# A two-layer GQA decode block: a reordered end, wider value steps and a table gelu

## The chip, the cores and the metric

The kernel runs on one NeuronCore of a Trainium2 chip. The metric is the device time of one execution in microseconds. Of the kernel before there are five runs: 306.32, 307.86, 307.25, 308.18 and 310.83 us, median 307.86. The profiled execution is the one of 306.32 us.

## The reference

Two layers of attention and of a gated FFN, with the same weights and the same caches in both layers, for one new token in each of four batch elements. x is 4 x 512, there are 32 query heads and 8 key/value heads of 128, and each cache holds 4096 positions per head; all in bfloat16.

```python
def _A_ref(x, k_cache, v_cache, wq, wo):
    q = (x @ wq) as heads
    k, v = caches, each head repeated 4 times
    scores = einsum("bhqd,bhkd->bhqk", q, k) * (Dh ** -0.5)
    o = einsum("bhqk,bhkd->bhqd", softmax(scores), v)
    return o @ wo
def _B_ref(x, w_gate, w_up, w_down):
    return (gelu(x @ w_gate) * (x @ w_up)) @ w_down    # tanh form, F = 1792

x = x + _A_ref(_layernorm(x), ...)      # twice over:
x = x + _B_ref(_layernorm(x), ...)      # attention, FFN, attention, FFN
```

## The kernel before, in words

**What moves.** K and V of one batch element are 8 MB each. The K tiles of an element stay in SBUF for both layers, so K is read once; V passes through seven buffers of 512 KB (`KV_BUFS`) and is read in both layers, but for two tiles of element 0 (`keep`). Weights are read once. All transfers are issued from SP, in the order in which the code calls `dma_start`; a V load waits until the matmuls that read its buffer's last tile are done, a K load until the scores that read the old tile are done.

**The pipeline over elements.** `attend(b2, b1)` runs the second layer's attention of element b2 = b beside the first layer's of element b1 = b + 1. Between two calls lies `dense(b, ...)`, the FFN of the first layer for one element: the second layer of an element needs its result. So the order for each element is: V steps of the first layer, out projection, `dense`, layer norm, q projection, K scores of the second layer; those scores free the K tiles for the next element's K loads. `attend_last` does the second layer of element 3, and the code behind it runs the second layer's FFN for all four elements at once and writes the output.

**V steps.** `Values.step` (L486) takes one V tile: 16 matmuls (L501), each with a 128 x 128 block of V as weights and four probability columns repeated `WIDE` = 8 times, 32 columns. A pass has 16 steps. The result's first copy is scaled into `OT_bf` on DVE (L509). `fill` in `dense` puts V steps of an earlier element between the FFN's stages, so that PE has work and V buffers come free. For element 0 there are no such steps, and `fill` calls `keep_clock(n)` (L342): n matmuls of 512 columns whose result nobody reads; `waits` gives the numbers. `down` (L349) repeats H's columns in the same manner, up to 32.

**The FFN and the norms.** `add_y` (L301) adds a result to x and accumulates its sum, `ln_square` (L165) the sum of squares; `ln_center` multiplies both with a constant matrix on PE to get mean and mean square in all partitions (L177) and subtracts the mean; `ln_rstd` (L193 to L208) finds 1/sqrt with integer arithmetic and two Newton steps on DVE. The gate and up projections (L314) leave rows that DVE turns into columns (L223). `gelu` is the tanh form: DVE operations around one ACT tanh (L328); `gate_up` multiplies with (tanh + 1) and with the up projection into `H_bf` (L340).

**The out projection.** Most heads go through `out_proj` into rows, which DVE turns and copies to `yc` (L269); `y_select` (L276) adds the rows up on PE (the row sums); the last heads are added directly by `out_proj_end` (L294).

**Softmax.** `soft` is a maximum on DVE and an exp on ACT (L418), `soft_turn` a turn on DVE (L426), `soft_swap` 16 matmuls and an ACT copy to `pe` (L445, L448), `soft_den` and `soft_recip` the denominators.

The schedule is written by hand: each engine runs its instructions in the order of the code. The functions that the change touches, with the profile's line numbers:

Of the kernel before, what the change touches and what calls it, by code (L numbers as in the profile page):

```python
# [15 lines left out]
P = 128  # L16
# [14 lines left out]
def kernel(  # L31
# [29 lines left out]
    WIDE = 8  # L61
# [40 lines left out]
    xo = state.tile([P, QS], BF16, name="xo")  # L102
    xr = state.tile([QS, P], BF16, name="xr")
# [6 lines left out]
    magic = const.tile([P, B], I32, name="magic")  # L110
    s32_f = const.tile([P, QS], FP32, name="s32_f")
# [30 lines left out]
    def build_consts():  # L142
        nc.vector.memset(mean_f[:], 1.0 / D)
        nc.vector.memset(magic[:], 0x5F3759DF)
        for r in ROWS:
            nc.vector.memset(r[:], 0.0)
        nc.vector.memset(qb[:], 0.0)
        nc.vector.memset(xo[:], 0.0)
        nc.vector.tensor_reduce(out=amask[:], in_=ident_bf[:].rearrange("p (a i) -> p a i", a=QD),
                                axis=AX.X, op=ALU.max)  # L150
        nc.vector.tensor_reduce(out=s32_f[:], in_=ident_bf[:].rearrange("p (a i) -> p i a", a=QD),
                                axis=AX.X, op=ALU.max)
        nc.vector.tensor_copy(out=t32_bf[:],
                              in_=s32_f[:].unsqueeze(1).broadcast_to([P, QD, QS]))
        nc.vector.tensor_reduce(out=hmask[:], in_=s32_f[:].rearrange("p (y h) -> p h y", h=rep),
                                axis=AX.X, op=ALU.max)
        nc.vector.scalar_tensor_tensor(
            out=dmask[:], in0=amask[:].unsqueeze(2).broadcast_to([P, GH, rep]), scalar=float(D),
            in1=hmask[:].unsqueeze(1).broadcast_to([P, GH, rep]), op0=ALU.mult, op1=ALU.mult)
# [12 lines left out]
    def ln_center(b0, nb):  # L172
        bs = slice(b0, b0 + nb)
        mv = small.tile([P, 2, nb], FP32, name="mv", tag="mv")
        if nb == 1:
            st = ps_sm.tile([P, 2, 1], FP32, name="st", tag="sm")
            nc.tensor.matmul(st.rearrange("p s o -> p (s o)"), lhsT=mean_f[:, :], rhs=sums[:],  # L177
                             start=True, stop=True)
            nc.vector.tensor_scalar(out=xn_bf[:, :, b0], in0=XX[:, 0, b0], scalar1=st[:, 0],
                                    scalar2=None, op0=ALU.subtract)  # L180
            nc.vector.tensor_copy(out=mv[:], in_=st[:])
            return mv
# [7 lines left out]

    def ln_rstd(nb, mv):
        msq = small.tile([P, nb], FP32, name="msq", tag="msq")
# [125 lines left out]
    def ffn_cols(rows, nb):  # L318
        return turn_rows(rows, KF * QS)[:, :, :nb]

    def gelu(nb, hg, rstd, sq, h):
# [8 lines left out]
                                       in1=spread_rstd(rstd, n, nb), op0=ALU.mult, op1=ALU.mult)  # L330

    def ffn_tiles(nb):
        sq = small.tile([P, KF, nb], FP32, name="sq", tag="sq")
        h = small.tile([P, KF, nb], FP32, name="h", tag="h")
        return sq, h, small.tile([P, KF, nb], BF16, name="H_bf", tag="H_bf")

    def gate_up(hu, sq, h, H_bf):
        nc.vector.scalar_tensor_tensor(out=sq[:], in0=sq[:], scalar=1.0, in1=h[:],
                                       op0=ALU.add, op1=ALU.mult)
        nc.vector.tensor_tensor(out=H_bf[:], in0=hu, in1=sq[:], op=ALU.mult)  # L340
# [8 lines left out]
    def down(nb, H_bf, between=()):  # L349
        n = WIDE * rep // nb  # L350
        y = ps_sm.tile([P, KD, n, nb], FP32, name="y", tag="sm")
        for c in range(KF):
            if c in between:
                keep_clock(between[c])
            for k in range(KD):
                nc.tensor.matmul(y[:, k], lhsT=wd_sb[:, c, k * P:(k + 1) * P],  # L356
                                 rhs=H_bf[:, c, :].unsqueeze(1).broadcast_to([P, n, nb]),
                                 start=(c == 0 and k == 0), stop=(c == KF - 1), skip_group_check=True)
        return y[:, :, 0]
# [103 lines left out]
    keep = {(0,) + u[2:] for u in value_order(0, 1)[:KEEP]}  # L463
# [18 lines left out]
    class Values:  # L482
# [3 lines left out]
        def step(self, count=1):  # L486
            for _ in range(min(count, VB - self.n)):
# [4 lines left out]
                pe, rden = self.prob[g]  # L492
                if self.n % (2 * NT) == 0:
                    self.ot = ps_ot.tile([P, 2, WIDE, rep], FP32, name="ot", tag="ot")
# [3 lines left out]
                for i in range(CH):  # L498
                    c = t * CH + i
                    rhs = pe[:, s, c, :].unsqueeze(1).broadcast_to([P, WIDE, rep])  # L500
                    nc.tensor.matmul(self.ot[:, s % 2], lhsT=v[:, i, :], rhs=rhs,  # L501
# [16 lines left out]
    def attend(b2, b1, next_q=None, rest=None):  # L518
# [78 lines left out]
        vals.step(2)  # L597
# [10 lines left out]
        vals.step(3)  # L608
        soft_turn(p0)
        if not first:  # L610
            for i in range(2):
                out_proj(rows, OT_bf, heads[i], hp, i == 0)
        pe, den = soft_swap(p0, p1p), soft_den(p0)
        if two:
            p1 = soft(sc2[1])
        prob1[gb] = (pe, soft_recip(den))
        vals.step(3)
        if two:
            soft_turn(p1)
            pe1, den1 = soft_swap(p1, p2p), soft_den(p1)  # L620
            prob2[gb] = (pe1, soft_recip(den1))
        if first:
# [7 lines left out]
            return (y, OT_bf, heads[3], hp), vals2  # L630
        vals.step()
        keep_clock(1)
        vals.step()
        out_proj(rows, OT_bf, heads[2], hp)
        vals.step()
# [9 lines left out]
    def attend_last(b2, next_q, rest):  # L645
# [27 lines left out]
        prob2[gb] = (soft_swap(p0, p2p), soft_recip(soft_den(p0)))  # L673
        out_proj(rows, OT2_bf, heads[0], hp, True)
# [7 lines left out]
        vals.step()  # L682
        y = y_select(yc, B)
        vals.step()
        return y, OT2_bf, heads[5], rep

    def dense(b0, nb, proj, fill, between=()):
# [4 lines left out]
        ln_square(b0, nb)  # L692
        mv = ln_center(b0, nb)
# [7 lines left out]
        gate_up(ffn_cols(ru, nb), sq, h, H_bf)  # L701
        fill(2)
        add_y(b0, nb, down(nb, H_bf, between))
# [4 lines left out]
    for b in range(B):  # L708
        if prev is None:
            waits = iter((1, 5, 6, 2, 1, 0, 3, 1))  # L710
# [3 lines left out]
        dense(b, 1, proj, fill, {KF // 2: 1, KF - 4: 1} if prev is None else ())  # L714
        ln_square(b, 1)
        fill(1)
        mv = ln_center(b, 1)
# [20 lines left out]
    def ffn_part(w_sb, h, c0, c1):  # L738
        for c in range(c0, c1):
            for k in range(KD):  # L740
# [6 lines left out]
    ln_square(0, B)  # L747
    mv = ln_center(0, B)
    banks = [new_rows(), new_rows()] + [new_scores(i).rearrange("p c j -> p (c j)")
                                        for i in range(NG)]  # L750
    hg, hu = [[t[:, :KF * B].rearrange("p (c j) -> p c j", j=B) for t in banks[i::2]]
              for i in range(2)]
    parts = [(0, KF // 2), (KF // 2, KF)]
    rstd = ln_rstd(B, mv)
    for i, (c0, c1) in enumerate(parts):
        ffn_part(wg_sb, hg[i], c0, c1)
    sq, h, H_bf = ffn_tiles(B)
    for i, (c0, c1) in enumerate(parts):
        gelu(B, hg[i][:, c0:c1], rstd, sq[:, c0:c1], h[:, c0:c1])
    for i, (c0, c1) in enumerate(parts):  # L760
        ffn_part(wu_sb, hu[i], c0, c1)
        gate_up(hu[i][:, c0:c1], sq[:, c0:c1], h[:, c0:c1], H_bf[:, c0:c1])
    y = down(B, H_bf)
    nc.vector.tensor_tensor(out=xo[:, :B * KD].rearrange("p (b k) -> p b k", k=KD),
                            in0=XX[:, 0], in1=y.rearrange("p k b -> p b k"), op=ALU.add)
    for a in range(QD):
        nc.vector.transpose(out=xr[:, a * QS:(a + 1) * QS], in_=xo[a * QS:(a + 1) * QS, :])
    nc.sync.dma_start(out=out.flatten_outer_dims().rearrange("b (k c) -> (b k) c", k=KD),
                      in_=xr[:B * KD, :])
# [30 lines left out]
```

## Time and profile before

| | |
|---|---|
| median of five runs | 307.86 us |
| profiled execution | 306.32 us |
| its span (first to last instruction) | 304.5 us |
| PE busy | 199.1 us, 65% |
| DVE busy | 172.3 us, 57% |
| ACT busy | 29.3 us, 10% |
| HBM read | 113.51 MB, 373 GB/s over the span |
| mean granted TensorE clock | 0.748 |

The page cuts the span into 40 slices of 7.6 us, each digit the busy share in tenths. PEclk is the granted clock of TensorE in tenths of full speed. The chain follows the work that ended last backwards, at each step to what released it; `SPq` is time in SP's queue, "issue" time in which an engine waited for nothing that the profile shows. PEld are the weight loads, which overlap the matmuls. In a timeline or group, `64x` or `x64` stands for so many instructions that are shown together, the time being that of the whole stretch.

### The profile page before, as it was taken

How to read it: one execution, taken by the hardware profiler on the slowest of the kernel's cores; microseconds unless marked ns; L12 is line 12 of the kernel's file. 1: busy time of each engine (PE TensorE's matmuls, PEld its weight loads, DVE VectorE, ACT ScalarE, POOL GpSimd, SP SyncE). 2: the span in 40 equal slices, each digit the busy share in tenths (PEclk: the TensorE clock that was granted, in tenths of full speed). 3: DMA queues.
4: the chain of work that ended last, by engine and by line, in shares of the span. 5: the costliest groups of instructions: out<-in, count | busy, mean ns of one | idle time of the engine just before them, and what ended most of it. 6: DMA issues, size and time to landing. Idle time of an engine off the chain costs nothing.

```text
span 304.5 us, 8771 instructions
## 1 busy us (share of the span) xinstructions
PE 199.1 (65%) x3865; PEld 118.1 (39%) x3873; DVE 172.3 (57%) x490; ACT 29.3 (10%) x71; POOL 0.7 (0%) x6
## 2 busy tenths in 40 slices
PE   1334385346767548788855387998562878988874
PEld 1011144112424125556431245564311555635654
DVE  6496841014258987465478953555799543545144
ACT  0003010000002021300100212001002130003100
POOL 0000000000000000000000000000000000000000
PEclk9998576557798558997965578799655795679685
DMA  7999999999958999999999999999999999999900
GB/s 246 429 410 423 413 419 414 361 372 393 389 180 321 405 413 418 419 415 416 402 408 405 418 414 418 417 411 405 399 403 412 418 418 418 374 342 418 405 23 3
DMA packets 34558, 114.09 MB, mean 375 GB/s; under 512 B 3156, under 2 KB 9048, under 8 KB 33496
## 3 DMA queue, kind: packets, MB, share of 16 engines
q1 hardware_dynamic: 34520, 113.53, 94.6%
q8 instruction: 30, 0.49, 0.6%
q14 instruction: 8, 0.07, 0.1%
HBM read 113.51 MB, written 0.00 MB: 373 GB/s over the span
## 4 chain that ended last, share of the span: by engine, by line
DMA 49%; PE 24%; DVE 15%; SPq 6%; issue 3%; ACT 1%; DVEq 0%; ACTq 0%
DMA v<-in_A_v_cache_dram 24%; DMA kt<-in_A_k_cache_dram 20%; PE ot L501 6%; DMA wd_sb<-in_B_w_down_dram 5%; PE sc L399 4%; SPq L134 3%; PE y L356 3%; DVE kt L388 2%; DVE rows L223 2%; PE rows L288 2%; PE rows L314 2%; PE rows L233 1%; DVE pp L426 1%; DVE qb L257 1%; SPq L135 1%
## 5 line engine op out<-in xcount | busy, mean ns | idle before, releaser
L501 PE MATMUL ot<-pe,v 128*128 128x32 bf16 x1920 | 65.0, 182 | 22.4 <-DMA v<-in_A_v_cache_dram 19.8
L501 PEld LDWEIGHTS <-v 128*128 128x128 bf16 x1920 | 58.1, 100 | 51.8 <-DMA v<-in_A_v_cache_dram 29.9
L388 DVE STREAM_TRANSPOSE kt<-kt 128x1024 f32<-128x1024 f32 x64 | 75.5, 1218 | 4.5 <-DMA kt<-in_A_k_cache_dram 4.3
L399 PE MATMUL sc<-kt,qb 128*32 128x512 bf16 x512 | 55.0, 482 | 18.3 <-DVE kt L388 14.3
L223 DVE STREAM_TRANSPOSE rows<-rows 128x512 f32<-128x512 f32 (+1 forms) x23 | 16.2, 706 | 30.7 <-PE rows L233 13.9
L399 PEld LDWEIGHTS <-qb 128*32 128x32 bf16 x512 | 16.3, 106 | 44.4 <-issue 18.9
L509 DVE TENSOR_TENSOR OT_bf<-ot,rden 128x8 bf16<-128x8 f32 (+1 forms) x40 | 6.5, 163 | 39.9 <-PE ot L501 39.7
L418 ACT ACTIVATE pp<-sc,nm 128x512 bf16<-128x512 f32 x16 | 11.0, 687 | 148.0 <-DVE junk L414 126.8
L445 PE MATMUL x<-pp,ident_bf 128*32 128x128 bf16 x256 | 7.6, 245 | 20.3 <-DVE pp L426 20.3
L288 PE MATMUL rows<-wo_sb,OT_bf 128*1 128x512 bf16 (+1 forms) x136 | 13.3, 482 | 7.3 <-DMA wo_sb<-in_A_wo_dram 6.3
L233 PE MATMUL rows<-wq_sb,xn_bf 128*1 128x512 bf16 (+1 forms) x160 | 14.1, 481 | 4.8 <-DMA wq_sb<-in_A_wq_dram 4.5
L405 DVE TENSOR_REDUCE m<-sc 128x1 f32<-128x512 f32 x16 | 10.8, 677 | 10.2 <-PE sc L399 10.2
L445 PEld LDWEIGHTS <-ident_bf 128*32 128x32 bf16 x256 | 5.6, 104 | 25.7 <-issue 23.4
L426 DVE STREAM_TRANSPOSE pp<-pp 128x512 bf16<-128x512 bf16 x16 | 11.2, 699 | 3.8 <-ACT pp L418 3.8
L254 PE MATMUL qe<-qm,t_bf 128*128 128x64 bf16 x16 | 3.4, 210 | 13.9 <-DVE qm L244 8.5
L356 PE MATMUL y<-H_bf,wd_sb 128*128 128x32 bf16 x280 | 9.7, 192 | 2.6 <-DVE H_bf L340 1.2
L448 ACT CAST pe<-x 128x512 bf16<-128x512 f32 x16 | 9.4, 585 | 18.9 <-PE x L445 18.9
L356 PEld LDWEIGHTS <-wd_sb 128*128 128x128 bf16 x280 | 9.1, 102 | 4.0 <-DMA wd_sb<-in_B_w_down_dram 2.0
L346 PE MATMUL sc<-wq_sb,ident_bf 128*128 128x512 bf16 x25 | 10.2, 481 | 0.1
L257 DVE TENSOR_TENSOR qb<-qe,amask 128x256 bf16<-128x256 f32 x16 | 6.8, 424 | 4.6 <-PE qe L254 4.6
L301 DVE SCALAR_TENSOR_TENSOR XX<-XX,y 128x4 f32<-128x4 f32 x8 | 1.3, 158 | 13.2 <-PE y L356 9.3
L328 ACT ACTIVATE sq<-sq 128x14 f32<-128x14 f32 (+1 forms) x6 | 1.3, 219 | 76.1 <-DVE sq L326 76.1
(83 smaller groups left out, 133.8 us busy)
## 6 DMA issues: line engine op xcount, KB each, us to landing
v<-in_A_v_cache_dram SPq DMA_DIRECT2D x117, 512.0 KB, 7.9
kt<-in_A_k_cache_dram SPq DMA_DIRECT2D x48, 512.0 KB, 10.1
kt<-in_A_k_cache_dram SPq DMA_DIRECT2D x8, 1024.0 KB, 15.9
wq_sb<-in_A_wq_dram SPq DMA_DIRECT2D x2, 2048.0 KB, 14.2
wo_sb<-in_A_wo_dram SPq DMA_DIRECT2D x4, 1024.0 KB, 12.0
kt<-in_A_v_cache_dram SPq DMA_DIRECT2D x8, 512.0 KB, 9.6
wg_sb<-in_B_w_gate_dram SPq DMA_DIRECT2D x1, 1792.0 KB, 13.5
wu_sb<-in_B_w_up_dram SPq DMA_DIRECT2D x1, 1792.0 KB
```

The lines of the kernel that those rows point to most:

```text
L223: nc.vector.transpose(out=rows[:, :n], in_=rows[:, :n])
L233: nc.tensor.matmul(rows[j * QS:j * QS + nb, :], lhsT=xn_bf[:, k, bs], rhs=w, start=(k == 0), stop=(k == KD - 1))
L288: nc.tensor.matmul(rows[r0:r0 + lhsT.shape[-1], :], lhsT=lhsT, rhs=wo_sb[:, i, :], start=(start and n < QD), stop=(stop and n >= hp - QD))
L346: nc.tensor.matmul(idle, lhsT=ident_bf[:, :], rhs=wq_sb[0][:, 0, :512], start=True, stop=True, skip_group_check=True)
L356: nc.tensor.matmul(y[:, k], lhsT=wd_sb[:, c, k * P:(k + 1) * P], rhs=H_bf[:, c, :].unsqueeze(1).broadcast_to([P, n, nb]), start=(c == 0 an ...
L388: nc.vector.transpose(out=words, in_=words)
L399: nc.tensor.matmul(sc[s * QS:(s + 1) * QS], lhsT=qb[:, w0:w0 + 2 * W], rhs=kt[:, :, be // 2, :, be % 2], start=(t == 0 and be == 0), stop= ...
L405: nc.vector.tensor_reduce(out=m[:], in_=sc.rearrange("p c j -> p (c j)"), axis=AX.X, op=ALU.max)
L418: nc.scalar.activation(out=pp[:], in_=sc[:], func=ACT.Exp, bias=nm[:, 0:1], scale=scale, accum_out=ls[:])
L426: nc.vector.transpose(out=flat, in_=flat)
L445: nc.tensor.matmul(x[a * QS:(a + 1) * QS, s], lhsT=ident_bf[:, s * QS:(s + 1) * QS], rhs=pT[:, a], start=True, stop=True, skip_group_check ...
L501: nc.tensor.matmul(self.ot[:, s % 2], lhsT=v[:, i, :], rhs=rhs, start=(c == 0), stop=(c == C - 1), skip_group_check=True)
```

## The change

It has these parts:

- V steps use 48 columns (`WIDE` = 12), and 64 (`FULL` = 16) in the last four steps of a first-layer pass. `H_bf` holds four equal copies for one element, and `down` uses 48 columns; at the very end it uses 4.
- Single-element norms: `ln_rstd_one` reads mean and mean square from PSUM and has eight DVE operations, with per-partition scalars; the copy to `mv` goes away. For element 0 (`ln_mean`) and at the end (`ln_end`), the mean's product stands ahead of the squares, and the mean square gets a product of its own.
- `gelu` takes over the product with (tanh + 1), ahead of the up rows' turn. At the end of the kernel, ACT's table function for the tanh gelu replaces the five operations; a dummy activation on `sums` in `attend_last` brings its table in ahead.
- Clock keepers: other numbers for element 0, two more ahead of `down` for elements 1 to 3, two ahead of the last chunk of `down` for element 0.
- In `attend`, the exp's turn stands directly behind the softmax, and the out projections stand one at a time between V steps.
- In `attend_last`, the row sums stand behind the last V step.
- The output is put together in 64 partitions by two adds and one turn, and leaves in 64 pieces of 64 bytes instead of 16 of 256 bytes.
- `keep` is written as an expression over all elements, with `KEEP` tiles for element 0 and none for the others.

```diff
-    WIDE = 8
+    WIDE, FULL = 12, 16
...
+    def ln_mean(b0):
+        st = ps_sm.tile([P, 1], FP32, name="st", tag="sm")
+        nc.tensor.matmul(st[:], lhsT=mean_f[:, :], rhs=sums[:, 0:1], start=True, stop=True)
+        ln_square(b0, 1)
+        nc.vector.tensor_scalar(out=xn_bf[:, :, b0], in0=XX[:, 0, b0], scalar1=st[:],
+                                scalar2=None, op0=ALU.subtract)
+        st2 = ps_x.tile([P, 1], FP32, name="st2", tag="x")
+        nc.tensor.matmul(st2[:], lhsT=mean_f[:, :], rhs=sums[:, 1:2], start=True, stop=True)
+        return st, st2
+
+    def ln_rstd_one(st):
...
+        nc.vector.tensor_scalar(out=nv[:], in0=mean, scalar1=mean, scalar2=ex2, op0=ALU.mult,
+                                op1=ALU.subtract)
+        nc.vector.tensor_scalar(out=nh[:], in0=nv[:], scalar1=0.5, scalar2=-0.5 * LN_EPS,
+                                op0=ALU.mult, op1=ALU.add)
...
+        for _it in range(2):
+            nc.vector.tensor_scalar(out=r2[:], in0=rstd[:], scalar1=rstd[:], scalar2=nh[:],
+                                    op0=ALU.mult, op1=ALU.mult)
+            nc.vector.tensor_scalar(out=rstd[:], in0=r2[:], scalar1=1.5, scalar2=rstd[:],
+                                    op0=ALU.add, op1=ALU.mult)
+    def ln_end(nb):
...
+        nc.tensor.matmul(st[0][:], lhsT=mean_f[:, :], rhs=XX[:, 0], start=True, stop=True)
+        ln_square(0, nb)
+        nc.tensor.matmul(st[1][:], lhsT=mean_f[:, :], rhs=XX[:, 1], start=True, stop=True)
+        nc.vector.tensor_reduce(out=mv[:, 0], in_=st[0][:], axis=AX.X, op=ALU.add)
...
+        nc.vector.tensor_reduce(out=mv[:, 1], in_=st[1][:], axis=AX.X, op=ALU.add)
...
+        nc.vector.scalar_tensor_tensor(out=sq[:], in0=sq[:], scalar=1.0, in1=h[:],
+                                       op0=ALU.add, op1=ALU.mult)
...
-        n = WIDE * rep // nb
-        y = ps_sm.tile([P, KD, n, nb], FP32, name="y", tag="sm")
+        n = WIDE if wide else 1
+        y = ps_sm.tile([P, KD, n, B], FP32, name="y", tag="sm")
...
+                wide = FULL if not last and self.n >= VB - 2 * NT else WIDE
-                    rhs = pe[:, s, c, :].unsqueeze(1).broadcast_to([P, WIDE, rep])
+                    rhs = pe[:, s, c, :].unsqueeze(1).broadcast_to([P, wide, rep])
...
         p0 = soft(sc1)
-        vals.step(3)
         soft_turn(p0)
-        if not first:
-            for i in range(2):
-                out_proj(rows, OT_bf, heads[i], hp, i == 0)
+        vals.step(2)
         pe, den = soft_swap(p0, p1p), soft_den(p0)
+        prob1[gb] = (pe, soft_recip(den))
+        vals.step(8 - vals.n)
         if two:
+            out_proj(rows, OT_bf, heads[0], hp, True)
             p1 = soft(sc2[1])
-        prob1[gb] = (pe, soft_recip(den))
         vals.step(3)
         if two:
             soft_turn(p1)
+            out_proj(rows, OT_bf, heads[1], hp)
...
+        vals.step(2)
+        out_proj(rows, OT_bf, heads[2], hp)
         vals.step()
         keep_clock(1)
-        vals.step()
-        out_proj(rows, OT_bf, heads[2], hp)
-        vals.step()
         out_proj(rows, OT_bf, heads[4], rep, False, True)
...
+        nc.scalar.activation(out=sums[:], in_=sums[:], func=ACT.Gelu_apprx_tanh)
...
         vals.step()
+        vals.step()
         y = y_select(yc, B)
-        vals.step()
...
+        if between:
+            mv = ln_mean(b0)
+        else:
+            ln_square(b0, nb)
+            mv = ln_center(b0, nb)
...
         fill(2)
+        if not between:
+            keep_clock(2)
...
-            waits = iter((1, 5, 6, 2, 1, 0, 3, 1))
+            waits = iter((1, 5, 8, 5, 2, 1, 4, 2))
-        dense(b, 1, proj, fill, {KF // 2: 1, KF - 4: 1} if prev is None else ())
+        dense(b, 1, proj, fill, {KF // 2: 1, KF - 4: 1, KF - 1: 2} if prev is None else ())
...
+    nc.vector.tensor_tensor(out=h[:], in0=hg, in1=rs, op=ALU.mult)
+    nc.scalar.activation(out=sq[:], in_=h[:], func=ACT.Gelu_apprx_tanh)
+    nc.vector.tensor_tensor(out=h[:], in0=sq[:], in1=rs, op=ALU.mult)
+    for u, c0 in zip(hu, (0, KF // 2)):
+        c1 = c0 + KF // 2
+        ffn_part(wu_sb, u, c0, c1)
+        nc.vector.tensor_tensor(out=H_bf[:, c0:c1], in0=u[:, c0:c1], in1=h[:, c0:c1], op=ALU.mult)
+    y = down(B, H_bf, wide=False)
...
+    for i in range(2):
+        ps = slice(i * hp, (i + 1) * hp)
+        nc.vector.tensor_tensor(
+            out=xo.rearrange("p (b k i) -> p i b k", k=KD, i=2)[:, i],
+            in0=XX[ps, 0], in1=y[ps].rearrange("p k b -> p b k"), op=ALU.add)
+    nc.vector.transpose(out=xr[:], in_=xo[:])
```

## The prediction

> **What bounds the kernel now.** I read the page's slices first, then its chain, then the stages in windows, then the end of the chain in order of time. In the slices, DMA stands at nine tenths or more nearly everywhere:
>
> ```profile
> PE   1334385346767548788855387998562878988874
> ...
> PEclk9998576557798558997965578799655795679685
> DMA  7999999999958999999999999999999999999900
> GB/s 246 429 410 423 413 419 414 361 372 393 389 180 321 405 413 418 419 415 416 402 408 405 418 414 418 417 411 405 399 403 412 418 418 418 374 342 418 405 23 3
> ```
>
> 114 MB at 415 GB/s are 275 us of the span of 304.5. An edit pays only where the stream stops or where nothing streams. The chain says the same (`DMA 49%; PE 24%; DVE 15%`): PE and DVE end last only in pieces. The windows show the holes (after the times: busy time of PE, PEld, DVE, ACT, POOL, then granted clock, DMA share, GB/s):
>
> ```profile
> 84.00:88.00 4.00, 2.33 (x28) 0.76 (x25) 2.47 (x10) 0.00 (x0) 0.00 (x0) 1.00 0.47 193
> 88.00:92.00 4.00, 3.27 (x57) 1.50 (x53) 2.40 (x7) 0.00 (x0) 0.00 (x0) 1.00 0.55 148
> 92.00:96.00 4.00, 2.42 (x67) 1.63 (x56) 2.74 (x7) 1.67 (x4) 0.00 (x0) 1.00 0.83 292
> ...
> 212.00:216.00 4.00, 2.09 (x50) 1.34 (x43) 1.39 (x6) 1.67 (x4) 0.00 (x0) 0.98 0.98 364
> ```
>
> A lack of (415 - x) GB/s over 4 us costs (415 - x) x 4 / 415 us: together 5.9 us after element 0 (hole A), 0.5 us at 212, and by the same rule 0.4 us at 148 to 156. The last hole shows with its cause, when the windows follow the clock:
>
> ```profile
> 250.00:263.60 13.60, 12.40 (x234) 7.34 (x235) 5.70 (x29) 0.21 (x1) 0.00 (x0) 0.50 1.02 413
> 263.60:270.40 6.80, 5.36 (x152) 4.22 (x152) 3.95 (x22) 0.00 (x0) 0.00 (x0) 1.00 0.95 303
> ```
>
> Element 3's FFN runs with PE full and the clock at half; V buffers come free late, and 6.8 us at 303 GB/s lose 1.8 us (hole B). All holes have one shape: the next loads wait until the FFN and the q projection have led to the K scores that free the key tiles. From DMA's end near 290 to 304.5 nothing streams:
>
> ```profile
> 291.95 0.24 DVE yc L269
> 292.23 0.26 PE y L276 x8
> 292.48 0.51 PE ot L501 x16
> 293.24 0.55 PE y L294 x16
> ...
> 297.35 0.20 DVE h L323
> ...
> 299.16 0.20 DVE H_bf L340
> 299.40 1.67 PE y L356 x56
> 301.30 0.20 DVE xr L767
> ```
>
> The last V step (292.48) is not late for its data but stands on PE behind the row sums (292.23), which wait for `yc`.
>
> **1. Clock and width (V and down steps of 48 columns, 64 in the last four of a first pass).** The clock changes on a grid of 3.41 us (263.6 up, 270.4 down, 273.8 up, 280.7 down, 287.5 up, 294.3 down). Adding up the columns of the matmuls in each such window, as a share of what full speed could stream: windows at full clock kept it at 0.36 or more and lost it at 0.33 or less. With V and down columns times 1.5, the losers at 137.3, 191.9, 267.0 and 277.3 (0.33, 0.31, 0.32, 0.28) come to 0.50, 0.41, 0.41, 0.38, and the half-speed window at 250.0 goes from 0.35 to 0.43.
> Price of width: five 512-column clock keepers took 1.25 us at full clock and 2.29 at half, one alone 0.38 and 0.59, so a column takes 0.22 / 512 = 0.42 ns or 0.83 ns. 48 columns need 20 or 40 ns. A 32-column V matmul comes every 28 ns at full clock (64 in 1.81 us) and 29 at half (64 in 1.87). No row has 48 columns: at full clock between 28 (streaming hides) and 35 (16 columns added on top), at half 40 to 42. I take 28 and 40, since the 28 ns is far above 32 x 0.42: free at full clock, +0.18 us per step at half.
>
> The Trainium skill, "TensorE: Matmul & The Clock Gate", Part 1 (the HAM clock gate), speaks against this term: it gives full clock after one busy window of some 3.4 us, however the time is filled. The row at 250 has PE busy 12.40 of 13.60 us with the clock at 0.50, so busy time alone does not decide here. By the page, width would change no clock, and the sum below would lose its clock terms, some 2.9 us.
>
> **2. Elements 1 and 2: -0.9 us.** At full clock the gate projection takes 0.93 us, at half 1.66 (elements 1 and 3). Four copies of H give `down` the V steps' layout: 56 matmuls at 28 ns against 1.91 us, -0.3. The rstd chain falls from 11 dependent DVE operations of 0.19 us to 8; those with a per-partition scalar cost more (0.23 to 0.24, rows L723 and L179, plus 0.04 to the next), so -0.2 to -0.6; I take -0.2. Against it: the product with (tanh + 1) now stands ahead of the second turn on DVE and waits for ACT, +0.1 with that turn queued behind; two keepers ahead of `down` (0.43 us) fit under the 0.4 us that PE waits for `H_bf`. So 0.4 us shorter in element 1 and over 1 us in element 2, where half clock went in two windows: both holes (0.4 and 0.5) close, and no more can be gained, as DMA is full around them. The exp's turn directly behind the softmax makes DVE wait about 0.7 us with OT writes behind it; V's arrival covers that (1.4 us of waiting at 250.2), otherwise it costs the 0.7.
>
> **3. Element 3: -1.9 us.** From the end of the out projection (256.15) to the first scores (270.08) are 13.9 us, in element 1 at mostly full clock 13.1. With -0.3 and -0.2 from part 2 and 0.5 from the stretch before (254.2 to 256.15 against 1.43 us), 1.8 us; the hole is 1.8. Scores and q behind it (half clock from 270.4) take 4.4 us up to `qe`, 3.1 in element 1, so PE reaches the last V tiles some 3 us earlier, which pays only down to the tiles' landing: -0.1 more on the path here and -0.7 in part 5.
>
> **4. Hole A: +0.3 us.** Keepers number 8 and 5 where 6 and 2 stood ahead of the up and down projections; these hide in waits for weights (2.0 and 1.1 us). Two new ones ahead of the last chunk of `down` do not: its data land by about 81.5, +0.3 at full clock (+0.6 at half). The mean ahead of the squares starts `xn_bf` 0.1 us earlier, but `am` (85.20) waits for rstd, whose input now comes 0.1 to 0.2 us later through a second matmul: that eats the 0.2 of the shorter chain. Four keepers instead of one ahead of the scores: 4 x 0.22 from 86.4 is 87.3, against 87.10, +0.2. `down`'s first 28 at 28 ns give back 0.2. Every term passes to the end, since the stream is full after it.
>
> **5. The end: -2.4 us.** Row sums behind the last V step: the step goes from 292.4 to 291.6, `yc` and OT then order on DVE, out projection 0.5 earlier. Backlog of PE at full clock in 280.7 to 287.5: two out projections of 8 at 0.6 instead of 1.0 us, -0.7 with the softmax before them. Mean ahead of squares: xn 0.3 earlier, which no one needs, since h waits for rstd (297.24); two fp32 products in a row and a third reduction put rstd at +0.15. Table gelu: from h (297.35) to `down` (299.40) were 2.05 us; now h 0.2, ACT 0.24, product 0.2, H 0.2 with four hand-overs of about 0.05: 1.05, -1.0. The up projection ends at about 298.4 and is just covered. Its table load (1.28 us, seen once at 26.15) stands behind the last `pe` copy, in 14.2 us of idle ACT; uncovered it would cost the 1.28. `down` with 4 columns, at 28 instead of 30 ns: -0.1. Two adds and one turn for one add and four turns: three operations of 0.2 instead of five, -0.4. The output leaves in 64 pieces of 64 bytes instead of 16 of 256: no row shows such; between 0 and one more landing of 1.4 us, I take +0.15 (the pieces run in parallel).
>
> By the Trainium skill, "ScalarE: Activation LUTs", What ACT_TABLE_LOAD costs, a switch is 2.66 us with its drain; here the next activation began 0.02 us behind the 1.28.
>
> What the diff does not do: the set of kept V tiles is the same two of element 0 in both versions, and SP issues its transfers in the same order, so that part is 0.
>
> **Sum.** -0.9 - 1.9 + 0.3 - 2.4 = -4.9 us. The profiled execution took 306.3 us (span 304.5, 1.8 around it), so 301.4. It is the fastest of five; their median stands 1.5 above. As median I forecast **303.0 us**.
>
> **Rivals.**
> *All ceilings reached* (301.3): 0.4 more from each of three rstd chains and 0.5 more of the backlog, 1.7 us beyond the sum. For it: PE comes 3 us earlier to the last tiles; against: rstd is only partly on the path. Chance 0.24.
> *The holes stay* (306.3): the clock drops in the same windows and hole B keeps its 1.8; only the end's fixed terms (-0.5 - 1.0 - 0.1 - 0.4 + 0.15 = -1.85) and hole A's +0.3 count. For it: records of some matmuls can be missing from my count of columns. Chance 0.16.
> *Width at half clock* (311.5, slower): the clock does not hold in the last three FFNs; some 18 V steps on their paths pay 0.18 each (3.2), two keepers 0.86 less the 0.4 that is covered in each (1.4), three `down` 56 x 6 ns (1.0), hole A 0.6: 6.2, less the end's 1.85 and 0.2 per rstd chain, +3.7. It decides from a share of columns below 0.36 in the window from 253.4. Against it: at half clock 48 columns fill 0.87 of what the window at 250 can stream, and windows at half clock with 0.73 or more mostly rose. Chance 0.09. Uncovered cases (table load, output, turn) take 0.02.
> The forecast itself has 0.49.
>
> A change of 1% is about what a measurement of this kernel can tell from none. Faster by more: 0.49 + 0.24 and a little of the third case, 0.75; within: 0.14; slower: 0.11. The range reaches from below the first rival to above the second, 299.3 to 307.2.
>
> **What would show it.** Right: clock near 1.0 from 253 to 294; the stage before the last scores without a dip under 390 GB/s; V matmuls 28 ns apart; no table load behind the last V step; under 1.2 us from h to `down`; 13 us from DMA's end to the end. Wrong: a V matmul above 35 ns at full clock, half clock in the last FFN, hole A longer than by 0.5 us, or an output that lands over 0.5 us later.

## The result, and the profile after

The changed kernel takes **311.02 us** (median of 27 runs, 307.8 to 314.6) against 308.14 us (48 runs) of the kernel before: ratio **1.0104, 95% interval 1.008 to 1.0128**. It is slower by about 3 us, where 303.0 us were forecast. Ratios use only a kernel's undisturbed runs; beside e13, e14 and e15 below, these are 6 of the 29 runs of the kernel before, its lowest ones. The profiled execution took 309.07 us, its span is 307.2 us, its mean granted clock 0.838 (0.748 before).

The page after, slices of 7.7 us, rows as before:

```profile
PE   1334377448776547879855588888564878987775
...
PEclk9999995556999657989998557999885579799995
DMA  6999999999959999999999999999999999999920
GB/s 241 426 412 423 408 410 406 352 372 391 381 192 353 403 410 380 355 372 410 406 409 408 407 408 406 407 409 407 408 407 409 408 387 356 393 408 395 411 106 3
```

Three things are to be seen. The clock is better, as forecast. The plateau is lower: where the stream runs without a break, before stood at 418 and after stands at 408, although no load was changed. And there is a new dip (380, 355, 372) where before had 415 to 419. In windows (busy time of PE, PEld, DVE, ACT, POOL, then granted clock, DMA share, GB/s):

```profile
84.00:88.00 4.00, 2.57 (x27) 0.75 (x30) 3.04 (x12) 0.00 (x0) 0.00 (x0) 1.00 0.73 289
88.00:92.00 4.00, 3.51 (x55) 1.60 (x59) 1.62 (x4) 0.00 (x0) 0.00 (x0) 1.00 0.44 119
92.00:96.00 4.00, 2.58 (x50) 1.32 (x43) 2.99 (x9) 1.67 (x4) 0.00 (x0) 1.00 0.91 298
116.00:120.00 4.00, 3.83 (x69) 2.42 (x64) 3.15 (x4) 0.00 (x0) 0.00 (x0) 0.66 1.01 370
120.00:124.00 4.00, 1.82 (x57) 1.56 (x56) 1.99 (x6) 1.08 (x3) 0.00 (x0) 1.00 0.99 393
124.00:128.00 4.00, 3.32 (x101) 2.33 (x101) 2.33 (x8) 1.67 (x4) 0.00 (x0) 1.00 0.95 328
128.00:132.00 4.00, 3.75 (x95) 2.67 (x96) 1.19 (x4) 0.58 (x1) 0.00 (x0) 1.00 0.99 338
132.00:136.00 4.00, 2.73 (x61) 2.06 (x60) 1.22 (x9) 0.00 (x0) 0.00 (x0) 0.97 0.99 384
212.00:216.00 4.00, 3.69 (x75) 1.75 (x63) 2.58 (x8) 0.36 (x1) 0.00 (x0) 1.00 1.03 410
256.00:260.00 4.00, 3.08 (x64) 1.84 (x62) 1.23 (x4) 0.00 (x0) 0.00 (x0) 1.00 0.95 326
```

The dip at 212 us is gone (410), and hole A is a little smaller. But 116 to 136 us now lose 2.3 us (every 2 us below 400 GB/s counted by what they lack to 408), and hole B has not closed: it lies at 248 to 264 us and still loses 1.6 us by the same rule, now with the clock at 1.00 from 251.8 to 262.1 us. The last V packet lands at 296.1 us instead of 291.0, and only 11.1 us follow it instead of 13.5. The timeline of the end after:

```profile
296.55 0.37 PE L554 MATMUL ot<-pe,v 128*128 128x48 bf16 x8 [0.27 <-DMA v<-in_A_v_cache_dram]
...
296.86 0.26 PE L326 MATMUL y<-yc,s_f 128*32 128x16 f32 x8
...
297.18 0.54 PE L344 MATMUL y<-OT_bf,wo_sb 128*128 128x4 bf16 x16
297.76 0.17 DVE L355 TENSOR_TENSOR XX<-XX,y 128x16 f32<-128x16 f32 x1 [0.63 <-PE y L344]
...
300.83 0.22 DVE L815 TENSOR_TENSOR h<-rows,rstd 128x56 f32<-128x56 f32 x1
301.08 0.25 ACT L816 ACTIVATE sq<-h 128x56 f32<-128x56 f32 x1 [13.39 <-DVE h L815]
...
301.93 1.63 PE L408 MATMUL y<-H_bf,wd_sb 128*128 128x4 bf16 x56
303.60 0.36 DVE L826 TENSOR_TENSOR xo<-XX,y 64x16 bf16<-64x16 f32 x2 [1.42 <-PE y L408]
303.99 0.20 DVE L829 STREAM_TRANSPOSE xr<-xo 64x32 bf16<-64x32 bf16 x1
304.23 0.63 SPq L830 DMA_DIRECT2D out_dram<-xr  x1
```

The last V step now waits for its data, from h to `down` pass 1.10 us, and the output's issue takes 0.63 us. So the end did become shorter, and the time was lost ahead of it.

### The profile page after: what moved, and what is told of

The parts are those of the page before. It is cut to its first block, busy times and chain, and to the rows that moved or that the text cites. A ratio compares the mean times of both kernels' runs of the same rounds, so it can differ in the third digit from the quotient of the medians.

```text
span 307.2 us, 8778 instructions
## 1 busy us (share of the span) xinstructions
PE 204.3 (67%) x3886; PEld 125.5 (41%) x3896; DVE 171.6 (56%) x458; ACT 30.6 (10%) x72; POOL 0.7 (0%) x6
## 4 chain that ended last, share of the span: by engine, by line
DMA 54%; PE 19%; DVE 13%; SPq 9%; issue 2%; ACT 1%; ACTq 0%
DMA v<-in_A_v_cache_dram 25%; DMA kt<-in_A_k_cache_dram 23%; PE ot L554 6%; PE sc L451 4%; DVE kt L440 4%; DMA kt<-in_A_v_cache_dram 3%; DMA wd_sb<-in_B_w_down_dram 3%; SPq L141 3%; SPq L135 3%; PE y L408 2%; PE rows L364 2%; DVE rows L273 1%; DVE m L457 1%; DVE pp L478 1%; ACT pp L470 1%
## 5 line engine op out<-in xcount | busy, mean ns | idle before, releaser
L554 PEld LDWEIGHTS <-v 128*128 128x128 bf16 x1920 | 65.9, 104 | 41.6 <-DMA v<-in_A_v_cache_dram 22.5
L554 PE MATMUL ot<-pe,v 128*128 128x48 bf16 (+1 forms) x1920 | 74.0, 195 | 12.5 <-DMA v<-in_A_v_cache_dram 10.5
L451 PE MATMUL sc<-kt,qb 128*32 128x512 bf16 x512 | 52.9, 462 | 21.0 <-DVE kt L440 17.4
L283 PE MATMUL rows<-wq_sb,xn_bf 128*1 128x512 bf16 (+1 forms) x160 | 12.9, 435 | 4.7 <-DMA wq_sb<-in_A_wq_dram 4.6
L398 PE MATMUL sc<-wq_sb,ident_bf 128*128 128x512 bf16 x40 | 13.1, 414 | 0.2
L408 PEld LDWEIGHTS <-wd_sb 128*128 128x128 bf16 x280 | 8.1, 97 | 3.3 <-DMA wd_sb<-in_B_w_down_dram 2.1
L408 PE MATMUL y<-H_bf,wd_sb 128*128 128x48 bf16 (+1 forms) x280 | 8.6, 180 | 1.2 <-DMA wd_sb<-in_B_w_down_dram 1.0
L488 DVE RECIPROCAL rden<-den 128x16 f32<-128x16 f32 x16 | 4.0, 250 | 8.8 <-PE den L483 8.3
## 6 DMA issues: line engine op xcount, KB each, us to landing
wg_sb<-in_B_w_gate_dram SPq DMA_DIRECT2D x1, 1792.0 KB, 13.5
```

Of the source, the lines that this page charges most:

```text
L283: nc.tensor.matmul(rows[j * QS:j * QS + nb, :], lhsT=xn_bf[:, k, bs], rhs=w, start=(k == 0), stop=(k == KD - 1))
L398: nc.tensor.matmul(idle, lhsT=ident_bf[:, :], rhs=wq_sb[0][:, 0, :512], start=True, stop=True, skip_group_check=True)
L451: nc.tensor.matmul(sc[s * QS:(s + 1) * QS], lhsT=qb[:, w0:w0 + 2 * W], rhs=kt[:, :, be // 2, :, be % 2], start=(t == 0 and be == 0), stop= ...
L554: nc.tensor.matmul(self.ot[:, s % 2, :wide], lhsT=v[:, i, :], rhs=rhs, start=(c == 0), stop=(c == C - 1), skip_group_check=True)
```

## The experiments

Ratios are to the kernel before, run beside on the same chip, with their 95% intervals. "Places" are the offsets of the V buffers and K tiles in bytes, modulo 256. The compiler gave these addresses to the tiles; the trace doesn't show them. "Pace" is worked out from the packets of the trace: the bytes are taken in the order of issue, and a load's own are divided by the time in which they came; upper quartile of the V loads and median of the K loads behind 100 us. Paces that differ by less than 1 GB/s count as equal.

| run | what it is | V, K place | V, K pace GB/s | median us | ratio |
|---|---|---|---|---|---|
| before | | 0, 160 | 420.1, 410.2 | 308.14 | 1 |
| after | | 96, 192 | 410.6, 409.9 | 311.02 | 1.0104 (1.008 to 1.0128) |
| e1 | after, attend order of before | 96, 192 | 410.6, 409.6 | 308.25 | 1.0033 (1.0001 to 1.0064) |
| e2 | after, 32 columns | 96, 192 | 410.9, 409.8 | 310.95 | 1.0119 (1.0066 to 1.0173) |
| e3 | before, new end | 96, 192 | 410.6, 409.6 | 309.55 | 1.0028 (0.9987 to 1.0069) |
| e4 | e1 with 32 columns | 96, 192 | 410.2, 409.9 | 308.56 | 1.0046 (1.0015 to 1.0077) |
| e5 | before, places moved | 32, 192 | 410.6, 409.9 | 309.68 | 1.0117 (1.0042 to 1.0191) |
| e6 | after, places of before | 0, 160 | 419.8, 410.9 | 308.32 | 1.0004 (0.9966 to 1.0041) |
| e7 | e3, places of before | 0, 160 | 419.8, 409.9 | 306.82 | 0.9948 (0.9899 to 0.9997) |
| e8 | e1, places of before | 0, 160 | 420.1, 410.2 | 304.28 | 0.9897 (0.9854 to 0.994) |
| e9 | e1, all places at 0 | 0, 0 | 420.1, 419.8 | 300.27 | 0.9722 (0.9676 to 0.9768) |
| e10 | e6, the moved V step put back | 0, 160 | 420.1, 409.9 | 306.35 | 0.9952 (0.9919 to 0.9985) |
| e11 | e6, only the moved V step kept | 0, 160 | 420.1, 410.9 | 306.99 | 0.9964 (0.992 to 1.0009) |
| e12 | before, V at 256 modulo 512 | 0, 160 | 420.1, 410.9 | 308.64 (1 run) | |
| e13 | before, all places at 0 | 0, 0 | 420.1, 419.8 | 305.05 | 0.9914 (0.9855 to 0.9974) |
| e14 | e9 with 32 columns | 0, 0 | 420.1, 419.8 | 302.42 | 0.9918 (0.9859 to 0.9977) |
| e15 | e9, norms and keepers of before | 0, 0 | 420.1, 419.8 | 303.97 | 0.984 (0.9758 to 0.9921) |
| e16 | before, V at 64 | 64, 160 | 410.2, 410.2 | 311.37 (1 run) | |
| e17 | e3, all places at 0 | 0, 0 | 420.1, 420.1 | 303.22 | 0.9752 (0.9682 to 0.9822) |
| e18 | e9 again | 0, 0 | 420.1, 420.1 | 301.45 | 0.9746 (0.9687 to 0.9805) |

By the medians (308.70 us for the kernel before, beside them) e13, e14 and e15 stand at 0.988, 0.980 and 0.985. I lean on the other series where it matters.

**First series: order, width or end.** The theory was that the new order in `attend` starves the V buffers, the rivals that the width costs the time or that the lower plateau is chance.

e1 undoes the order:

```diff
-        vals.step(2 if first else 1)
+        vals.step(2)
...
         p0 = soft(sc1)
-        soft_turn(p0)
-        vals.step(2)
+        vals.step(3)
+        soft_turn(p0)
+        if not first:
+            for i in range(2):
+                out_proj(rows, OT_bf, heads[i], hp, i == 0)
```

and likewise the lines behind it.

> The changed kernel with the attend order of the kernel before: two V steps ahead of the first scores of the second group, three between softmax and turn, the out projections of the first two heads together behind the turn. Theory ORDER (the V steps that were moved behind the softmax chain free V buffers late, and the stream starves): the dips at 116 to 136 us and 248 to 264 us of the trace after (2.3 and 1.7 us lost) go; 4.0 us less than the changed kernel, about 307.0 us, ratio to the kernel before about 0.996. Theory WIDTH (48 columns cost time at half clock and draw the rate of the stream down): no change, about 311 us, dips as they are. Theory CHANCE (the 2-us rate of the full stream is 407.6 GB/s after against 413.7 before, about 3 us over 200 us, and that is only a difference between runs): dips go, but the kernel before, run beside it, shows the lower rate too.

e2 is the changed kernel with `WIDE, FULL = 8, 8`.

> The changed kernel with 32 columns in all V steps and in the single-element down projections. Theory ORDER: the dips stay; the clock falls to half in some windows where it held, about 311 to 312 us. Theory WIDTH: some 18 half-clock V steps of the path get back 0.18 us each, 3.2 us, and if the width lowers the rate of the stream, it goes from 407 back to about 413 GB/s, another 3 us: 305 to 308 us.

e3 takes only the end of the changed kernel (row sums behind the last V step, `ln_end`, the table gelu, two adds and one turn; `H_bf` keeps four equal copies, `down` its 32 columns).

> The kernel before with only the new end: row sums behind the last V step, mean ahead of squares at the end, table gelu, one output turn. Nothing ahead of the last scores changes. From the stream's end to the last instruction were 13.6 us before and 11.2 us in the changed kernel: 2.4 us less, about 305.7 us, ratio 0.992, by every theory. If it is not faster, the shorter tail of the changed kernel came from its late stream and not from the new end.

e4 is e1 with `WIDE, FULL = 8, 8`.

> Both undone: attend order of the kernel before and 32 columns; the norms, the gelu, the clock keepers and the end stay as changed. Theory ORDER: like the first run of this series, about 307, or 1 us less if the width costs something at half clock. Theory WIDTH: like the second. If both are wrong and keepers or norms cost the time, this stays at about 311 us against 305.7 us of the run with only the new end.

Measured: 1.0033, 1.0119, 1.0028, 1.0046. The order costs some 0.7%, the width nothing that these runs can tell. What no theory had: e3, whose tail behind the last V packet is 11.5 us, is not faster than before. The windows of e1 show why (same columns):

```profile
116.00:120.00 4.00, 3.05 (x78) 1.96 (x75) 2.90 (x5) 0.00 (x0) 0.00 (x0) 1.00 1.03 408
120.00:124.00 4.00, 3.00 (x80) 2.01 (x77) 3.05 (x13) 1.74 (x5) 0.00 (x0) 1.00 1.03 410
124.00:128.00 4.00, 3.10 (x100) 2.65 (x100) 1.20 (x4) 1.60 (x4) 0.00 (x0) 1.00 1.03 408
128.00:132.00 4.00, 3.42 (x69) 2.01 (x70) 1.07 (x3) 0.00 (x0) 0.00 (x0) 1.00 1.03 407
132.00:136.00 4.00, 3.61 (x99) 2.65 (x98) 2.27 (x14) 0.00 (x0) 0.00 (x0) 1.00 1.02 405
```

The dip is gone, but the full stream stands at 408, not at the 413 to 419 of before, with the DMA engines as busy. All four kernels, and the changed one, share this lower plateau, e3 too, whose V steps, norms and softmax ahead of the last scores are those of before. Besides the new end, which lies behind this stretch, they share the place of the tiles: the changed kernel's new 4-byte constant `magic1` takes 32 bytes ahead of all weights and K tiles, and `xr` takes 64 instead of 256 bytes per partition ahead of the V buffers. So the V buffers went from a multiple of 512 bytes to 96 modulo 256.

**Second series: only the places.** e5 is the kernel before with 32 bytes of padding; in e6 to e8, `magic1` stands with the state tiles and 160 bytes of padding restore the V buffers' and K tiles' addresses.

```diff
     dmask = const.tile([P, GH, rep], FP32, name="dmask")
+    const.tile([P, 16], BF16, name="pad_c")
```

> The kernel before with nothing changed but places in SBUF: 32 bytes of padding per partition ahead of the weights, so that the seven V buffers start at 32 instead of 0 modulo 512 bytes, the K tiles at 448 instead of 416. No instruction differs. Theory PLACE (a load streams at 420 GB/s into a buffer that starts at a multiple of 512 bytes and at 409 into one that does not; the changed kernel's new small tiles moved the V buffers off such an address): the V loads fall from 420 to about 409 GB/s; 65.5 MB of V take 160.2 instead of 156.0 us, so at most 4.2 us longer, about 3.5 us since not every V load runs at the full rate: ratio about 1.011. Theory CHANCE (the rate differed between the runs) and theory ORDER alone: ratio 1.000.

> The changed kernel with only the places in SBUF restored: the V buffers at 0 modulo 512 bytes, weights and K tiles at 416, as in the kernel before. Theory PLACE: V loads at 420 GB/s again, about 3.5 us less: ratio to the kernel before from 1.010 to 0.999, or a little less where later V steps hide part of it in waits. Theory CHANCE: stays at 1.010.

> The kernel before with only the new end, and the V buffers where they were in the kernel before. Theory PLACE: the 2.2 us that the tail is shorter (13.6 to 11.4 us in the profiles) now reach the time: ratio about 0.992 to 0.993. Theory CHANCE: stays at 1.003.

> The changed kernel with the attend order of the kernel before and the V buffers where they were. Theory PLACE with ORDER: from 1.0033 to about 0.991. If the closed clock holes of my forecast (2.8 us) are there at all, this is faster than the run with only the new end and the same places, by up to 0.9%; if wide steps, norms and keepers are worth nothing, it equals it.

Measured: 1.0117, 1.0004, 0.9948, 0.9897. The page of e5, which has not one instruction that the kernel before lacks (it counts 8 more because the trace before has 3865 matmul records and this one 3873; the other engines' counts are equal):

```profile
span 306.9 us, 8779 instructions
...
GB/s 247 428 412 424 406 410 405 352 372 394 382 212 332 413 410 408 407 405 366 382 408 408 411 407 405 408 406 406 408 406 409 408 407 386 397 373 409 397 42 3
```

Moving buffers by 32 bytes turns the 418 into 408 and costs 1.2% (0.4 to 1.9); giving the changed kernel the old places takes 1.0% from it. 65.5 MB of V take 3.6 us more at 410.6 than at 420.1 GB/s, and 1.0 to 1.2% are 3.1 to 3.6 us. CHANCE is out. The weight loads from V on PE take 100 ns on average in e5 and in the kernel before: what became slower is the transfer, not its reader.

e12 and e16 look for the step, with 256 and 64 bytes of padding ahead of the V buffers alone.

> The kernel before with 256 bytes of padding behind the state tiles: only the V buffers (and small tiles) move, to 256 modulo 512 bytes; K stays at 416. To see which step of places the rate follows. If multiples of 256 bytes are enough, V loads stay at 420 GB/s; if 512 are needed, they fall to about 409.

> The kernel before with the V buffers at 64 modulo 512 bytes, K as it was. V at 256 modulo 512 kept 420 GB/s, at 32 it fell to 409. If multiples of 64 bytes are enough, V loads run at 420 GB/s; if 256 are needed, at about 409 to 410, and the stream ends some 3 us later than in the profile before.

V at 256 modulo 512 keeps 420.1 GB/s; at 64 it falls to 410.2. A multiple of 256 bytes is enough and one of 64 is not; 128 was not tried.

The Trainium skill, "DMA: Bandwidth & Descriptors", How a descriptor splits into AXI transactions, says that a descriptor that does not start at a multiple of 256 bytes begins with a transaction from the boundary below, and that what lies between costs beats of 32 bytes (it speaks of what a transaction reads; here it is the place written that moves). The runs agree on the 256. They don't agree on the price: by the page, 4096 bytes at 32, 96 and 160 would pay 1, 3 and 5 beats in 128 (an estimate of 0.8, 2.3 and 3.9%), and measured were 2.3, 2.3 and 2.3% (410.6 and 410.6 of 420.1 for V, 410.2 of 419.8 for K).

**Third series: which half of the order, and K.** The new order has two halves: the turn directly behind the softmax, and one V step that moved from ahead of the second group's first scores to behind them. e10 puts back the V step, e11 keeps only that move. The edit of e10 against e6:

```diff
-        vals.step(2 if first else 1)
+        vals.step(2)
```

> The changed kernel, V buffers placed as before, with one line of the attend order undone: two V steps instead of one ahead of the first scores of the second group. With the whole order undone the ratio went from 1.0004 to 0.9897. Theory MOVED STEP (the V step that went behind the softmax chain frees its buffer some 4 us later, and everything behind it follows): nearly the whole 1.1% comes back, 0.990 to 0.993. Theory TURN (the exp's turn directly behind the softmax makes PE and DVE wait with no V step to run): stays at 0.997 to 1.000.

> The complement: V buffers placed, softmax, turns and out projections in the order of the kernel before, but one V step ahead of the first scores of the second group and four between softmax and turn. Theory MOVED STEP: 0.997 to 1.000, as with the whole changed order. Theory TURN: 0.990, as with the whole order undone.

Measured: 0.9952 and 0.9964, between the 1.0004 of the whole new order and the 0.9897 of the old one. Neither expectation holds: each half costs about 0.5%, though the intervals of both runs reach to those of the whole order and of none. The timelines show both halves. Before, from the last scores to the second softmax's products:

```profile
119.45 1.67 PE L501 MATMUL ot<-pe,v 128*128 128x32 bf16 x48
...
121.05 1.03 PE L288 MATMUL rows<-wo_sb,OT_bf 128*1 128x512 bf16 x16
...
121.85 0.71 DVE L426 STREAM_TRANSPOSE pp<-pp 128x512 bf16<-128x512 bf16 x1 [0.53 <-ACT pp L418]
...
122.61 0.41 PE L445 MATMUL x<-pp,ident_bf 128*32 128x128 bf16 x16 [0.53 <-DVE pp L426]
```

and after:

```profile
120.14 0.98 PE L554 MATMUL ot<-pe,v 128*128 128x48 bf16 x32
...
122.53 0.71 DVE L478 STREAM_TRANSPOSE pp<-pp 128x512 bf16<-128x512 bf16 x1 [0.91 <-ACT pp L470]
123.29 0.41 PE L497 MATMUL x<-pp,ident_bf 128*32 128x128 bf16 x16 [2.18 <-DVE pp L478]
...
123.88 0.96 PE L554 MATMUL ot<-pe,v 128*128 128x48 bf16 x32
```

Before, three V steps and two out projections cover the softmax, and PE waits 0.53 us for the turn. After, two steps cover it, PE stands 2.18 us, and the next steps, which free V buffers, follow only behind the products, at 123.88: the two that ran at 119.86 and 120.55 us before come 4.0 and 3.7 us later. The load that waits for the second of them is issued at 124.89 instead of 121.15 us. SP's waits from 116 to 136 us, before and after (us in total, times, longest):

```profile
SPq L479 <- PE ot L501: 12.3, 13, 2.8
...
SPq L531 <- PE ot L554: 12.7, 10, 3.2
```

With equal places the lag stays. At 164 us the V loads of e6 are issued 2.8 us behind those of e8 (166.89 against 164.07), and the last V packet lands 4.5 us later (295.87 against 291.35): most of the loss is made in this first stretch. A dip in one profile is weak evidence by itself. The profile of e7, which has the old order, is of a run of 309.47 us (its median is 306.82) and shows one too, 263 GB/s at 128 to 132 us. The order's cost rests on the times and on these late loads.

e9 is e1 with all weights, K tiles and V buffers at a multiple of 512 bytes:

```diff
     dmask = const.tile([P, GH, rep], FP32, name="dmask")
+    const.tile([P, 48], BF16, name="pad_c")
...
-    magic1 = const.tile([P, 1], I32, name="magic1")
+    magic1 = state.tile([P, 1], I32, name="magic1")
...
     qb = state.tile([P, W + NK * 2 * W], BF16, name="qb")
+    state.tile([P, 288], BF16, name="pad_s")
```

> The changed kernel with the attend order of the kernel before and with weights, K tiles and V buffers all at 0 modulo 512 bytes (96 bytes of padding behind the constants, 576 behind the state tiles). Theory PLACE, whole: K loads rise from 410 to 420 GB/s as well; 33.5 MB of K take 2.0 us less, 12 MB of weights 0.7 us less where they run at the full rate: 1.5 to 2.5 us below the run with only the V buffers placed, ratio about 0.983. If the rate depends on something else than the place (V against K, the stage of the program), it stays at 0.990.

Measured: 300.27 us, 0.9722; K now runs at 419.8. It beats both kernels, and by more than expected: 1.7% below e8, where K and weights explain 0.9. The rest is not explained. By the rule above, e9's profile loses 2.6 us in dips behind 100 us and e8's 3.7, but the profile of e18, the same kernel as e9, loses 5.8 in a run of 304.48 us. The page of e9:

```profile
span 298.0 us, 8776 instructions
...
GB/s 236 429 421 429 416 420 418 384 402 407 407 181 350 406 419 418 417 415 417 412 414 418 418 417 412 410 416 412 414 417 418 417 417 415 352 409 392 416 122 3
```

**Fourth series: what the other parts are worth on a full stream.** e13 gives the kernel before the places of e9; e14 and e15 take the width, or norms, product and keepers, out of e9; e17 has only the new end, e18 is e9 beside it.

> The kernel before with nothing but places: weights, K tiles and V buffers all at 0 modulo 512 bytes (V was there already). K loads from 410 to 420 GB/s: 33.5 MB take 2.0 us less, weights 0.7 us less at most. Theory PLACE: 1.5 to 2.5 us faster, ratio 0.992 to 0.995. What is left to the 0.9722 of the changed kernel with old attend order and the same places is then the worth of the other parts together: 2.0 to 2.3%, 6 to 7 us.

> The ninth kernel (attend order of the kernel before, all places at 0 modulo 512) with 32 columns instead of 48 and 64. My forecast gave the width and clock most of 2.9 us: then the ratio goes from 0.972 to 0.981. If the width is worth nothing, as the slow-stream runs suggest (1.0046 against 1.0033), it stays at 0.972 to 0.976.

> The ninth kernel with the single-element norms, the place of the (tanh + 1) product and the clock keepers of the kernel before; width, end and places as in the ninth. My forecast gave norms and product 0.1 to 0.3 us in each of three elements and charged the keepers of element 0 with 0.3: near 0 to 0.5 us, ratio 0.972 to 0.974. If they are worth more than the width, 0.976 or above.

> The kernel before with only the new end, and all places at 0 modulo 512 bytes. Beside the kernel before with the same places (0.991, 305.05 us) it tells the worth of the end, forecast at 2.2 to 2.4 us: about 302.7 us, ratio 0.984. Beside the next run it tells the worth of width, norms, product and keepers together, forecast at 2.5 us: 0.8% above it. If the end alone brings all, both are equal at 0.972 to 0.978; the intermediate runs without the width (302.42 us) and without norms and keepers (303.97 us) speak for a difference of 2 to 4 us.

> The ninth kernel once more, beside the run above on one chip: 300.3 us and 0.972 the first time. If that was a lucky chip, it comes out at 0.980 to 0.985, level with the versions that lack the width or the norms.

e13 (0.9914) agrees with K and weights gaining 0.9%. e14 and e15 lie 0.6 and 1.1% above e9 by their medians, but on another chip. On one chip, e17 and e18 differ by 1.8 us in their medians and by nothing in their ratios (0.9752 and 0.9746, each with 0.6 to 0.7% to both sides). Two earlier pairs ask the same with other places: e7 and e8 differ by 2.5 us in their medians and by 0.5% in their ratios, e3 and e1 by 1.3 us and by nothing; the medians favour the fuller kernel each time. So width, norms, product and keepers together are worth between nothing and some 2.5 us; the runs cannot say more. e9's first 0.9722 was confirmed at 0.9746.

## Why the prediction was wrong

Forecast were -4.9 us, measured about +3: 8.1 us apart, as 1.0104 against the 0.9842 that 303.0 us are of 307.86. They come apart into three parts. That the third rival's 311.5 us lies near the 311.02 measured is luck: it needed half clock in the last three FFNs, and the mean clock rose from 0.748 to 0.838.

**The places (3.1 us, e6 against after).** The prediction had no such step: it took 415 GB/s of the profile before as the stream's own rate and the new tiles `magic1` and `xr` as free. That was the first failure, and no rival had it.

**The order of `attend` (3.3 us, e8 against e6).** Part 2 named one half of it, the turn, and costed it at nothing: "V's arrival covers that (1.4 us of waiting at 250.2), otherwise it costs the 0.7". The other half, the V step that moved, stands in the kernel but neither in the list of parts nor in the prediction: a term left at nothing without a reason. For the half that was named, the step that failed is the cover. It was read from one stretch in which V was late, and laid over 116 to 136 us, where V was there and PE's V steps were themselves the cover. The 0.7 us was also the wrong price: what counts is not DVE's wait but the buffers freed 4 us late.

**The rest (1.7 us, e8's 0.9897 against 0.9842).**

- Part 5, the end: forecast -2.4. Its anchor was the profile before, with 13.5 us behind the last V packet. The other four profiles with the old end have 12.5 to 12.9, the 15 with the new one 11.0 to 11.8. So the end gives some 1.2 us, and e7 (-0.5%, 1.6 us) agrees. Pairs whose loads run at the same pace, but on different chips, give more, each with some 0.9% to both sides: 0.9% for e3 against e5, 1.6% for e17 against e13. By terms, against the end of e5, shown here:

```profile
294.13 0.26 PE L277 MATMUL y<-yc,s_f 128*32 128x16 f32 x8
...
294.96 0.39 PE L502 MATMUL ot<-pe,v 128*128 128x32 bf16 x8 [0.26 <-DMA v<-in_A_v_cache_dram]
...
296.22 0.17 DVE L306 TENSOR_TENSOR XX<-XX,y 128x16 f32<-128x16 f32 x1 [0.66 <-PE y L295]
...
299.75 0.19 DVE L324 TENSOR_TENSOR h<-rows,rstd 128x28 f32<-128x28 f32 x1
...
301.81 1.66 PE L357 MATMUL y<-H_bf,wd_sb 128*128 128x32 bf16 x56 [0.82 <-DVE H_bf L341]
...
304.58 0.35 SPq L769 DMA_DIRECT2D out_dram<-xr  x1
```

  The row sums are over by 294.4 and the last V step waits for its data even in the old order: the -0.5 and the -0.7 for the backlog are 0 here. They were true of the profile before, where the step starts 1.45 us behind the last V packet; in e5, e12 and e13 it starts 0.4 to 0.5 us behind it, as after, and in e16 0.8. The chain from XX to h falls from 3.53 to 3.07 us (+0.15 was forecast), the gelu from 2.06 to 1.10 (-1.0 forecast, right), `down` stays, adds and turns give 0.45 (0.4, right). From the output's issue to the end pass 2.98 instead of 2.37 us: +0.6, where 0.15 was taken.
- Parts 1 to 3, the clock: the mechanism was half right. The clock held nearly where it was said to (full from 251.8 to 262.1 and from 265.5 to 299.6 us), and the width did it: with 32 columns and nothing else changed, e2 has a mean clock of 0.72 to 0.76 in its runs, the changed kernel 0.79 to 0.85. V matmuls start 25 ns apart at full clock with 32 and with 48 columns and 31 with 64, at half 27, 40 and 53 ns (medians): the price was right for 48 columns, but 64 are not free. The rule of columns is less sharp than part 1 has it. By the same count, a window of the profile before lost the clock at 0.38 (75.9 us), and after, two windows kept it at 0.23 (159.7 and 224.5 us) and one lost it at 0.35 (132.4 us). And the better clock bought no time that the runs show (1.0104, and 1.0119 for e2). "The hole is 1.8" and goes, the -1.9 of part 3, failed: hole B stands at 1.6 us with the clock at 1.00, and in e9 the stream falls to 324 GB/s at 256 to 260 us with the clock at full from 249.5 to 290.5. Its depth does not follow the clock alone; what sets it is left open. For parts 2 and 3 together stand -2.8 in the sum; measured were nothing to -2.5 us for everything but the end and the order.
- Part 4: the +0.3 came, though the hole's size does not show it. From `down`'s first matmul to the first scores pass 8.3 us (79.65 to 87.96) instead of 8.0 (79.06 to 87.10), and SP still stands for these scores: the K loads behind them are issued from 89.10 instead of 88.21 us. The other 0.6 us lie ahead of `down`, which waits for its weights; with the places of before (e6) it begins at 79.11. By the forecast's rule hole A lost 5.2 us instead of 5.9 because the loads ahead of it ended later too (289 instead of 193 GB/s from 84 to 88 us).
- The table load (1.28 us at 286.19) was hidden, and the kept tiles changed nothing, as said.

## What to carry to other kernels

In a kernel that streams, look up the address of every DMA destination, before and after a change: two small tiles ahead of the buffers cost 3 us, more than the 1.2 us by which the profiles show the end shorter, and padding to multiples of 512 bytes (for V, 256 were enough) was worth 0.9% (0.3 to 1.5) to the unchanged kernel. A better clock for the matmuls is no gain by itself where the loads set the time. V steps between a softmax and its products are not idle fill; they free the buffers that the next loads wait for, so a step moved behind the products is paid in the stream. And an end that is measured on one profile should be measured on several: 0.6 to 1.0 us of the 13.5 was that execution's own.

## What was not expected of the hardware

- A load into SBUF ran at 420 GB/s where each partition's 4096 bytes started at a multiple of 256 bytes, and at 410 where they started at 32, 64, 96, 160 or 192 bytes behind one, with DMA engines busy in both (DMA share 1.03 and 1.03 in the windows). What inside the transfer costs the 2.3% is not shown.
- An output of 64 pieces of 64 bytes took 0.63 us to issue and ended 2.98 us behind the issue's start; 16 pieces of 256 bytes took 0.35 and 2.37 us.
- At full clock a V matmul took 25 ns from start to start with 32 as with 48 columns, and 31 ns with 64.
